# Another order for the opening of an attention and MLP kernel, with the first MLP weight loaded in four places

## Chip, cores and metric

One core of one Trainium2 chip runs the whole program. The metric is the device time of one execution in microseconds; the lower, the better. Shown for the kernel before are three runs: 415.26, 416.80 and 418.37 us, median 416.8 us.

## What is computed

Per batch and head: q and k are divided by their root mean square along the 64 dimensions and weighted by a gain; the scores are their products over 8; a softmax and a product with v follow. The heads are laid side by side (768 columns), and an MLP with a leaky activation ends the work.

```python
def rmsnorm(x, g):
    return x / np.sqrt(np.mean(x * x, axis=-1, keepdims=True) + 1e-06) * g
# q, k, v: (8, 12, 448, 64)
scores = 1/8 * np.matmul(rmsnorm(q, g_q), rmsnorm(k, g_k).transpose(0, 1, 3, 2))
attn = softmax(scores)
x = np.matmul(attn, v).transpose(0, 2, 1, 3).reshape(3584, 768)
h = x @ w_in                                      # 768 x 2048
g = np.maximum(h, 0.0) + alpha * np.minimum(h, 0.0)
out = g @ w_out                                   # 2048 x 768
```

## The kernel before, in words

Attention goes in 24 units, three for each of the eight batches; a unit `y` holds two heads of each half of the heads (the text says "unit 3" for y = 3, "q3" and "k3" for its inputs). The MLP goes batch by batch: 16 column blocks of 128 of the first weight (`up(b,ft)`, `slope`, `larger`), then output tiles of 128 tokens (`down` and, from tile 6, a scheme with fewer products).

For units 0 to 8 the steps of one unit, each on a fixed engine, are: `load_qk(y)` on the queue of SyncE (SP); `square` on GpSimd (POOL; L382, unit 0 and q1 on ScalarE); `reduce` on VectorE (DVE; L401); `root`, two short ScalarE (ACT) instructions (L422, L423); `scale` (L442, on VectorE for units 1, 2 and q3, else on GpSimd); `turn`, 14 transposes on TensorE (PE; L566) and two copies out of PSUM on VectorE (L573, L575); seven `score` steps (L594, four matmuls each in the early units) and seven `soft` (the exponential, L608, 0.8 to 0.9 us each on ScalarE); `den`, `log`, `invert` (the sum of the exponentials and its reciprocal), `attend` (the product with v, L619) and `times` (L715). `follow` is a one-column copy on GpSimd. `spin` is matmuls without use for the result.

`load_w_in(c)` issues from GpSimd four loads of 32 partitions by 512 columns (L345) for column quarter c, and, for c = 0 and c = 2, four more loads with rows 512 to 767 of a column half (L353). So column blocks 0 to 3 need load_w_in(0), blocks 4 to 7 need load_w_in(0) and (1), blocks 8 to 11 need load_w_in(2), blocks 12 to 15 need load_w_in(2) and (3). `begin(ft)` does the part of `up(0,ft)` that needs only units 0 and 1. `load_v` and `load_w_out` are issued by GpSimd as well.

The order of everything is written out by hand in one string, `PLAN`: the steps are emitted in its order, and each engine runs its own instructions in that order. Where an instruction waits, all behind it on its engine wait. The GpSimd loads are numbered round robin over eight completion semaphores (DMASW0 to DMASW7 in the built program): a load waits until the load eight places before it on that queue has landed. The loads of SP go round robin over eight others in the same way.

Buffers: q and k of units 0, 1, 3, 4, 6, 7 lie in four rotating buffers (`nat`), so load_qk(3) waits for the last reader of unit 0's, which is `scale`; units 2, 5 and 8 share one place in `arena`. v has one buffer. PSUM has two score buffers, one spare buffer (a last argument 1 in `score`, `up`, `den`, `down` and others changes which of them is taken) and two single banks for the MLP and the transposes.

Of the kernel before, what the change touches and what calls it, by code (L numbers as in the profile page):

```python
# [32 lines left out]
reduce(2,q,1) soft(0,3) score(0,1,0) scale(1,k) scale(1,q) soft(0,4) score(0,2,0) soft(0,2)  # L33
reduce(2,k) score(0,6,1) turn_one(1,q) soft(0,1) turn_one(1,k) score(1,0,1) score(1,3,0) spin(1)
score(1,2,0) soft(0,6) root(2) soft(1,0) load_qk(4) soft(1,3) scale(2,k) scale(2,q) soft(1,2)
score(0,5,1) score(1,1,0) soft(0,5) soft(1,1) score(1,5,0) turn(2) soft(1,5) score(1,6,1)
soft(1,6) reduce(3,q,None) score(1,4,0) score(2,0,0) square(3,k) soft(1,4) den(0+1,0) follow(1,k)
# [3 lines left out]
times(0+1,0,0) turn(3) score(2,5,0) square(4,k) load_qk(6) reduce(4,q,None) soft(2,3) soft(2,2)  # L41
soft(2,5) den(2,0) log(2) reduce(4,k,None) invert(2) attend(2,0,1) score(3,0,1) square(5,q)
square(5,k) times(2,0,0) score(3,1,0) begin(0) reduce(5,q) square(6,q) soft(3,0) begin(1)
up(0,0,0) load_w_out(0) reduce(5,k) up(0,1,0) begin(2) begin(3) root(4) up(0,2,0) up(0,3,1)
up(0,4,0) scale(4,q) slope(0,0) soft(3,1) larger(0,0) score(3,2,0) score(3,6,0) slope(0,1)
load_qk(7) follow(2,k) larger(0,1) slope(0,4) slope(0,2) slope(0,3) larger(0,4) up(0,5,0)
larger(0,2) larger(0,3) root(5) soft(3,6) slope(0,5) soft(3,2) larger(0,5) up(0,6,0) scale(4,k)
turn(4) scale(5,q) up(0,8,0) score(4,0,0) slope(0,6) score(4,1,1) square(6,k) larger(0,6)
slope(0,8) score(3,5,0) up(0,9,0) load_w_out(1) scale(5,k) soft(4,0) square(7,q) larger(0,8)
up(0,11,0) load_qk(8) score(4,2,0) score(3,3,0) soft(3,5) load_v(1) square(7,k) up(0,7,1)  # L50
soft(4,1) slope(0,9) up(0,10,0) reduce(6,q) square(8,q) reduce(6,k) load_w_out(2) soft(4,2)
up(0,12,0) slope(0,11) larger(0,9) soft(3,3) score(3,4,0) slope(0,10) score(4,3,0) larger(0,11)
larger(0,10) slope(0,7) larger(0,7) up(0,13,0) soft(3,4) slope(0,12) larger(0,12) turn(5)
up(0,14,0) square(8,k) soft(4,3) score(4,6,0) slope(0,13) score(4,4,1) root(6) slope(0,14)
larger(0,13) up(0,15,0) scale(6,q) reduce(8,q) soft(4,4) score(5,4,0) larger(0,14) scale(6,k)
score(5,0,1) reduce(7,q) slope(0,15) larger(0,15) down(1,0,0) score(5,2,1) score(4,5,0) soft(4,6)
soft(5,0) soft(5,4) soft(5,2) score(5,1,0) soft(4,5) down(0,0,0) turn(6) load_w_out(3) den(3+4,1)
reduce(7,k) attend(3+4,0,0) score(5,5,0) score(5,6,0) soft(5,1) mix_weights(0,1) log(3+4)
invert(3+4) soft(5,5) soft(5,6) mix_weights(0,3) attend(3+4,1,0) score(6,0,1) score(5,3,0)
soft(6,0) score(6,4,0) down_end(0,0) down(2,0,0) soft(5,3) root(7) scale(7,q) load_qk(9) soft(6,4)  # L60
scale(7,k) den(5,0) attend(5,0,1) down_end(1,0) mix_weights(0,2) times(3+4,0,0) times(3+4,1,0)
times(3+4,1,1) load_qk(10) log(5) down(0,1,0) reduce(8,k) invert(5) down_end(2,0) times(5,0,1)
times(5,0,0) times(5,0,3) times(5,0,2) score(6,5,1) mix_weights(0,0) score(6,1,0) down_end(0,1)
score(6,6,0) soft(6,5) turn(7) up(1,1,1) square(9,q) down(1,1,0) root(8) reduce(9,q) soft(6,6)
score(6,3,1) score(7,0,0) slope(1,1) score(6,2,0) up(1,2,0) up(1,0,0) soft(6,1) soft(7,0)
soft(6,3) square(9,k) up(1,3,1) up(1,4,0) slope(1,2) slope(1,0) larger(1,1) down_end(1,1)
reduce(9,k) root(9) larger(1,2) load_qk(11) larger(1,0) slope(1,3) scale(8,q) soft(6,2) up(1,7,0)
slope(1,4) larger(1,3) larger(1,4) scale(8,k) score(7,4,0) slope(1,7) larger(1,7) up(1,5,1)
scale(9,q) turn(8) score(7,5,0) soft(7,4) score(7,1,0) up(1,6,0) square(10,q) slope(1,5)
larger(1,5) up(1,10,0) soft(7,5) soft(7,1) up(1,8,1) scale(9,k) up(1,9,0) reduce(10,q)  # L70
score(7,2,0) slope(1,6) slope(1,10) larger(1,6) mix_weights(1,1) score(7,6,0) slope(1,8)
slope(1,9) soft(7,6) up(1,12,1) up(1,11,0) soft(7,2) square(10,k) up(1,13,0) larger(1,8)
larger(1,10) slope(1,12) score(7,3,0) larger(1,9) up(1,14,1) slope(1,11) slope(1,13)
# [1030 lines left out]
```

## Time and profile before

| | |
|---|---|
| median of three runs | 416.8 us |
| the profiled execution | 416.01 us |
| its span in the trace | 414.2 us, so 1.81 us lie around it |
| PE busy in the span | 397.6 us (96%) |
| DVE, ACT, POOL busy | 267.9, 269.9, 301.2 us |
| first score matmul | 14.43 us |
| begin(0), the first MLP matmul | 45.06 us |
| mean granted TensorE clock | 0.988 |

Times inside an execution are microseconds from the start of the span. In the timeline, a line is: start, duration, engine, source line, operation, output<-inputs, count; what stands in brackets is the idle time of that engine just before, and what ended it. In the table of stretches a line gives the length, then busy time and count for PE, PEld (weight loads), DVE, ACT and POOL, then the granted TensorE clock, the busy share of the 16 DMA engines and GB/s. The chain of waits is the work that ended last, followed back: start, length, what.

### The profile page before, as it was taken

To read this page: it belongs to the slowest core of one execution; us is meant where nothing else is said; L and a number is where in the kernel's file an instruction comes from. 1 tells how busy PE (TensorE), PEld (TensorE's weight loads), DVE (VectorE), ACT (ScalarE), POOL (GpSimd) and SP (SyncE) were. 2 spreads that over 40 slices of the span, in tenths; PEclk is the share of its full clock that TensorE was granted. 3 is DMA by queue.
4 is the path that set the end of the run, shared out by engine and by line. 5 is a ranking of instruction groups with operands and counts; after the bars stand their busy time and mean duration, and the time that the engine had idled before them with its cause. 6 is when DMAs were issued, how large, how long until landed. Compare 5 with 4: busy or idle time off the path is not lost.

```text
span 414.2 us, 11992 instructions
## 1 busy us (share of the span) xinstructions
PE 397.6 (96%) x5083; PEld 211.3 (51%) x5083; DVE 267.9 (65%) x479; ACT 269.9 (65%) x405; POOL 301.2 (73%) x200
## 2 busy tenths in 40 slices
PE   7785999999999999999999999999999999999995
PEld 3342444555445555555455445545555455655664
DVE  3936776566766777677867758886659545654422
ACT  5594688757786776667897887876875885235110
POOL 7849998297888698998695996489497709600780
PEclk9897999999999999999999999999999999999999
DMA  8999599697867594749872695794707000230143
GB/s 254 244 273 167 111 245 188 128 234 189 161 133 185 147 216 99 174 117 200 212 172 58 157 218 147 151 217 106 161 21 143 24 0 23 59 78 0 34 101 95
DMA packets 37221, 58.39 MB, mean 141 GB/s; under 512 B 4768, under 2 KB 28976, under 8 KB 37168
## 3 DMA queue, kind: packets, MB, share of 16 engines
q1 hardware_dynamic: 23232, 45.43, 42.9%
q0 software_dynamic: 13536, 11.81, 19.3%
q8 instruction: 39, 0.64, 0.7%
q10 hardware_dynamic: 400, 0.39, 0.3%
q14 instruction: 14, 0.11, 0.1%
HBM read 58.40 MB, written 11.01 MB: 168 GB/s over the span
## 4 chain that ended last, share of the span: by engine, by line
PE 89%; DMA 4%; POOL 3%; DVE 2%; ACT 1%; issue 1%; POOLq 0%
PE hT L732 26%; PE hTa L732 9%; PE sc L594 8%; PE op L798 7%; PE qx L860 5%; PE av L619 5%; PE qc L860 4%; PE qz L860 4%; PE oq L860 3%; PE dn L619 3%; PE qxa L860 3%; DMA w_in_sb<-in_moe_w_in_dram 2%; PE avb L619 2%; PE oqm L860 2%; DMA nat<-in_q_dram 1%; PE tps L566 1%
## 5 line engine op out<-in xcount | busy, mean ns | idle before, releaser
L608 ACT ACTIVATE expT<-sc 128x896 f16<-128x896 f32 x168 | 146.1, 916 | 41.7 <-PE sc L594 39.9
L732 PE MATMUL hT<-xT,w_in_sb 128*128 128x448 f16 x558 | 115.7, 353 | 0.3 <-DVE xT L715 0.2
L732 PEld LDWEIGHTS <-w_in_sb 128*128 128x128 f16 x768 | 73.0, 98 | 73.1 <-issue 8.8
L429 POOL TENSOR_TENSOR qs<-nat,rr 128x896 f16<-128x896 f32 x30 | 65.6, 2218 | 26.7 <-ACT rr L423 23.2
L772 ACT ACTIVATE gT<-hT,cols 128x448 f16<-128x448 f32 x92 | 58.4, 635 | 39.6 <-PE hT L732 38.5
L778 DVE TENSOR_TENSOR gT<-hT,gT 128x448 f16<-128x448 f32 x93 | 57.4, 620 | 38.0 <-ACT gT L772 37.2
L594 PE MATMUL sc<-qT,kT 64*32 64x448 f16 (+1 forms) x1092 | 50.1, 359 | 8.2 <-ACT expT L608 6.6
L371 POOL TENSOR_TENSOR nat<-nat 128x896 f32<-128x896 f32 x30 | 50.6, 1694 | 8.8 <-DVE gT L778 4.4
L860 PEld LDWEIGHTS <-gT 128*128 128x128 f16 x352 | 33.4, 98 | 25.5 <-issue 4.1
L732 PE MATMUL hTa<-xT,w_in_sb 128*128 128x448 f16 x198 | 42.9, 353 | 0.0
L715 DVE TENSOR_TENSOR xT<-av,rden 64x448 f16<-64x448 f32 (+1 forms) x37 | 27.2, 736 | 12.9 <-ACT rden L677 6.9
L594 PEld LDWEIGHTS <-kT 64*32 64x32 f16 (+1 forms) x1092 | 16.8, 94 | 36.7 <-issue 27.8
L848 POOL TENSOR_TENSOR gs<-gT 128x1024 f16<-128x1024 f16 x4 | 8.5, 2126 | 36.7 <-DVE gT L778 36.7
L392 DVE TENSOR_REDUCE sp<-nat 128x28 f32<-128x896 f32 x30 | 32.1, 1071 | 2.0 <-DMA nat<-in_k_dram 2.0
L798 PE MATMUL op<-w_out_sb,gT 128*128 128x384 f16 x176 | 30.3, 326 | 0.2 <-DVE xT L715 0.2
L772 ACT ACTIVATE gT<-hTa,cols 128x448 f16<-128x448 f32 x33 | 21.0, 635 | 10.5 <-PE hTa L732 10.0
L778 DVE TENSOR_TENSOR gT<-hTa,gT 128x448 f16<-128x448 f32 x33 | 20.4, 619 | 10.6 <-ACT gT L772 10.2
L619 PEld LDWEIGHTS <-vt 64*32 64x32 f16 x1344 | 19.6, 92 | 12.4 <-issue 2.6
L798 PEld LDWEIGHTS <-gT 128*128 128x128 f16 x192 | 18.3, 98 | 14.5 <-issue 3.0
L619 PE MATMUL av<-expT,vt 64*32 64x448 f16 x896 | 24.3, 350 | 0.0
L856 POOL TENSOR_TENSOR gT<-gT 128x1024 f16<-128x1024 f16 x11 | 23.4, 2131 | 0.0
L860 PEld LDWEIGHTS <-arena 128*128 128x128 f16 x136 | 12.6, 98 | 10.5 <-issue 2.3
(152 smaller groups left out, 575.4 us busy)
## 6 DMA issues: line engine op xcount, KB each, us to landing
nat<-in_q_dram SPq DMA_DIRECT2D x60, 216.0 KB, 4.0
nat<-in_k_dram SPq DMA_DIRECT2D x60, 216.0 KB, 5.1
out_dram<-osb SPq DMA_DIRECT2D x107, 96.0 KB, 3.2
vt<-in_v_dram POOLq DMA_DIRECT2D x8, 672.0 KB, 8.2
w_in_sb<-in_moe_w_in_dram POOLq DMA_DIRECT2D x24, 128.0 KB, 7.1
w_out_sb<-in_moe_w_out_dram POOLq DMA_DIRECT2D x4, 768.0 KB, 8.2
nat<-in_k_dram SPq DMA_DIRECT2D x6, 448.0 KB, 6.2
nat<-in_q_dram SPq DMA_DIRECT2D x5, 448.0 KB, 6.3
```

Of the source, the lines that this page charges most:

```text
L371: nc.gpsimd.tensor_mul(out=sqs[y, nm], in0=t[:, :, :HD], in1=t[:, :, :HD])
L392: nc.vector.tensor_reduce(out=parts[y][:, ts("qk".index(nm), 4 * J), :1], in_=sqs[y, nm], axis=AXIS_X, op=ALU.add,)
L429: nc.gpsimd.tensor_mul(out=t.rearrange("p j d n -> p n j d"), in0=nat[y, nm][:, :, :HD].rearrange("p (n j) d -> p n j d", j=J), in1=r.unsq ...
L594: nc.tensor.matmul(out=sc[ds(64 * g + m * c, m), par, :S].rearrange("p (j c) -> p j c", j=J), lhsT=kT[ds(64 * par, 64), j, g, ts(c, m)], r ...
L608: nc.scalar.activation(out=expT[y][:, j], in_=scs[y, j][:, :, :S], func=AF.Exp, scale=QK_SCALE, bias=EXP_BIAS,)
L619: nc.tensor.matmul(out=accs[g][ds(32 * n, 32), :S], lhsT=weights(g, y, par, c, j), rhs=expT[y][ds(64 * g, 64), j, par, :], start=(j == 0), ...
L715: nc.vector.tensor_mul(out=o, in0=p, in1=q)
L732: nc.tensor.matmul(out=hT[:, :S], lhsT=w_in_sb[:, block_of(g, i), ts(ft, 128)], rhs=xT[b][:, g, i, :], start=(i == 0 and g == 0), stop=(i ...
L772: nc.scalar.activation(out=g, in_=hT[:, :S], func=AF.Copy, scale=alpha_sb[:, ft : ft + 1])
L778: nc.vector.tensor_max(out=g, in0=hT[:, :S], in1=g)
L798: nc.tensor.matmul(out=op[:, :OH], lhsT=gT[:, ft, ts(tile % J, 128)], rhs=w_out_sb[:, ft, ts(oh, OH)], start=(ft == 0), stop=(ft == NF - 1),)
L860: nc.tensor.matmul(out=bank[:, c], lhsT=g[:, ft], rhs=v[:, ft, c], start=(first and ft == 0), stop=(ft == HF - 1), skip_group_check=True,)
```

## The change

Only `PLAN` changes. Both strings hold the same 1324 steps with the same arguments, apart from the bank argument. The order of the first 49 lines (up to slope(1,13), in the MLP of batch 1) is another; the rest keeps its order, with 17 bank arguments changed. In the four load_w_in, what stands between them in GpSimd's order is:

- before: load_w_in(1), square(1,k), load_v(0), follow(0,k), square(2,q), square(2,k), load_w_in(0), load_w_in(2), square(3,q), square(3,k), follow(1,k), load_w_in(3), scale(3,k), square(4,q), square(4,k), square(5,q), square(5,k), square(6,q), load_w_out(0), scale(4,q), ...
- after: load_w_in(1), square(1,k), load_v(0), square(2,q), follow(0,k), load_w_in(3), square(2,k), follow(1,k), square(3,q), square(3,k), square(4,q), load_w_in(0), scale(3,k), square(5,q), square(5,k), square(4,k), load_w_in(2), scale(4,q), scale(4,k), square(7,q), load_w_out(0), load_w_out(1), follow(2,k), scale(5,k), load_v(1), square(6,q), load_w_out(2), scale(5,q), load_w_out(3), ...

SP loads the units in the order 3, 4, 5, 7, 6, 8, 9, 10 in place of 3 to 10. The four mix_weights(0,p) go from between turn(6) and turn(7) to behind turn(8). The new string is one line shorter, so line numbers behind it are one lower.

```diff
-opening() part_square(q,0:1,0:7,act) part_square(q,1:2,0:7,act) part_reduce(q,0:1,0:7) spin(2,0)
-part_reduce(q,1:2,0:7) part_root(q,0:7) part_square(k,0:2,0:3,act) part_scale(q,0:7,7,pool)
-part_reduce(k,0:2,0:3) part_square(k,0:2,3:7,act) square(1,q) load_w_in(1) spin(1)
-part_reduce(k,0:2,3:7) part_root(k,3:7) reduce(1,q) square(1,k) part_root(k,0:3) gains()
-part_turn(q,r0-7) load_qk(3) spin(1,0) part_scale(k,0:3,3,vec) part_turn(k,r0-3)
-part_scale(k,3:7,4,vec) part_copy(q,0:7,vec) part_turn(k,r3-7) load_v(0) reduce(1,k) follow(0,k)
-square(2,q) part_copy(k,0:3,vec) part_copy(k,3:7,vec) root(1) square(2,k) score(0,0,0) soft(0,0)
-reduce(2,q,0) score(0,4,1) load_w_in(0) load_w_in(2) square(3,q) score(0,3,0) spin(1)
...
-soft(2,0) log(0+1) load_qk(5) score(2,1,0) spin(1) reduce(3,k,0+1) attend(0+1,1,0) score(2,6,0)
-score(2,4,1) attend(0+1,0,1) soft(2,1) root(3) score(2,3,1) invert(0+1) scale(3,q) score(2,2,0)
-load_w_in(3) soft(2,4) soft(2,6) times(0+1,1,0) times(0+1,1,1) scale(3,k) square(4,q)
...
+opening() part_square(q,0:1,0:7,act) part_reduce(q,0:1,0:7) spin(2,0) part_square(q,1:2,0:7,act)
+part_reduce(q,1:2,0:7) load_qk(3) part_root(q,0:7) part_square(k,0:2,0:3,act)
+part_reduce(k,0:2,0:3) part_scale(q,0:7,7,pool) part_square(k,0:2,3:7,act) part_reduce(k,0:2,3:7)
+load_w_in(1) square(1,k) part_root(k,0:3) spin(1) part_scale(k,0:3,3,vec) square(1,q) load_qk(4)
+part_root(k,3:7) reduce(1,q) gains() part_turn(k,r0-3) part_turn(q,r0-7) part_scale(k,3:7,4,vec)
+load_v(0) square(2,q) part_copy(q,0:7,vec) reduce(1,k) part_copy(k,0:3,vec) part_turn(k,r3-7)
+part_copy(k,3:7,vec) score(0,0,0) score(0,3,0) root(1) follow(0,k) score(0,4,1) scale(1,q)
+load_w_in(3) scale(1,k) reduce(2,q,0) score(0,6,0) soft(0,0) turn_one(1,q) turn_one(1,k) soft(0,4)
+score(0,1,1) score(1,0,0) spin(1) score(0,5,0) soft(0,6) square(2,k) soft(0,3) score(1,3,1)
+score(0,2,1) reduce(2,q,1) score(1,1,0) soft(0,1) follow(1,k) reduce(2,k) soft(1,0) score(1,5,0)
+square(3,q) soft(1,3) reduce(3,q,None) spin(1) root(2) square(3,k) scale(2,q) soft(0,5) spin(1,0)
+score(1,6,1) score(1,2,0) soft(0,2) soft(1,1) soft(1,5) reduce(3,k,0+1) scale(2,k) turn(2)
+square(4,q) load_w_in(0) soft(1,6) root(3) soft(1,2) score(1,4,0) spin(1) score(2,0,1) scale(3,k)
+soft(1,4) score(2,1,0) load_qk(5) den(0+1,1) soft(2,0) soft(2,1) square(5,q) score(2,6,1) log(0+1)
+score(2,3,0) soft(2,6) attend(0+1,1,0) attend(0+1,0,1) invert(0+1) scale(3,q) times(0+1,1,0)
+soft(2,3) score(2,2,1) times(0+1,1,1) score(2,4,0) times(0+1,0,0) reduce(4,q,None) turn(3)
+score(2,5,1) soft(2,2) square(5,k) reduce(5,q) soft(2,4) soft(2,5) den(2,1) attend(2,0,1) log(2)
+invert(2) square(4,k) times(2,0,0) reduce(4,k,None) score(3,0,1) soft(3,0) load_qk(7) score(3,2,0)
+begin(0) begin(1) reduce(5,k) begin(2) root(4) up(0,0,0) up(0,1,0) begin(3) load_qk(6) slope(0,0)
+load_w_in(2) up(0,2,0) larger(0,0) scale(4,q) slope(0,1) soft(3,2) up(0,4,0) up(0,3,1) larger(0,1)
+up(0,5,0) score(3,6,0) slope(0,3) scale(4,k) square(7,q) load_w_out(0) larger(0,3) slope(0,4)
+slope(0,2) load_w_out(1) score(3,1,0) larger(0,2) larger(0,4) soft(3,6) soft(3,1) slope(0,5)
+root(5) turn(4) up(0,6,0) score(3,4,0) slope(0,6) score(4,0,0) up(0,10,1) soft(3,4) follow(2,k)
...
```

More of the change, by code (lines that the diff above doesn't have):

```diff
@@ L31 @@
-square(2,q) part_copy(k,0:3,vec) part_copy(k,3:7,vec) root(1) square(2,k) score(0,0,0) soft(0,0)
-reduce(2,q,0) score(0,4,1) load_w_in(0) load_w_in(2) square(3,q) score(0,3,0) spin(1)
[L33 to L36, printed above, removed]
@@ L43 @@
[L43 to L48, printed above, removed]
@@ L49 @@
[L49 to L72, printed above, removed]
@@ new lines @@
+reduce(6,q) soft(4,6) larger(0,13) slope(0,14) up(0,15,0) soft(5,6) score(5,5,1) score(4,5,0)
+reduce(6,k) slope(0,15) score(5,4,0) load_qk(9) soft(4,5) larger(0,14) larger(0,15) root(6)
+reduce(7,k) square(8,q) down(0,0,0) score(5,1,1) score(5,2,0) score(4,4,0) soft(5,5) soft(5,4)
+load_qk(10) soft(5,2) down(1,0,0) scale(6,q) scale(6,k) soft(5,1) root(7) soft(4,4) reduce(8,q)
+turn(6) down_end(1,0) den(3+4,1) attend(3+4,0,1) down_end(0,0) score(5,3,1) square(8,k) log(3+4)
+score(6,0,0) soft(5,3) attend(3+4,1,0) down(2,0,1) den(5,1) invert(3+4) attend(5,0,1) scale(7,k)
@@ new lines @@
+soft(6,0) times(3+4,0,0) times(3+4,1,0) reduce(8,k) root(8) times(3+4,1,1) scale(7,q) score(6,6,1)
+down_end(2,0) log(5) score(6,5,0) down(0,1,0) invert(5) times(5,0,3) times(5,0,0) soft(6,5)
+scale(8,q) soft(6,6) times(5,0,1) score(6,4,1) times(5,0,2) score(6,1,0) down_end(0,1)
+score(6,2,0) soft(6,4) turn(7) soft(6,2) soft(6,1) square(9,q) up(1,1,1) down(1,1,0) score(7,0,0)
+slope(1,1) larger(1,1) up(1,0,1) reduce(9,q) slope(1,0) up(1,2,0) scale(8,k) soft(7,0) square(9,k)
+down_end(1,1) reduce(9,k) up(1,3,0) slope(1,2) up(1,4,1) larger(1,0) up(1,7,0) score(7,4,0)
```

41 lines of the change are left out of this document (25 added, 16 removed).

## The prediction, made before the changed kernel was timed

> **What bounds the kernel now.** I read the stretches first, to see where PE is not full, then GpSimd's timeline there, then the chain of waits that leads out of it. The stretches:
>
> ```profile
> 25.00:30.00 5.00, 4.11 (x91) 1.97 (x94) 0.75 (x2) 4.97 (x7) 2.15 (x4) 1.00 1.12 260
> 30.00:35.00 5.00, 3.19 (x119) 1.69 (x104) 2.04 (x3) 0.18 (x1) 4.45 (x6) 1.00 1.09 227
> 35.00:40.00 5.00, 2.38 (x21) 1.54 (x21) 3.65 (x6) 4.51 (x7) 4.99 (x6) 0.60 0.85 116
> 40.00:45.00 5.00, 5.00 (x128) 2.16 (x126) 2.99 (x4) 2.45 (x3) 5.00 (x4) 0.72 0.58 187
> 45.00:50.00 5.00, 5.00 (x31) 2.57 (x28) 4.42 (x6) 3.45 (x7) 4.98 (x6) 1.00 0.33 33
> 150.00:200.00 50.00, 50.00 (x668) 26.57 (x666) 37.77 (x72) 34.77 (x52) 46.64 (x26) 1.00 0.72 155
> ```
>
> From 45 us on PE is busy almost without a break at full granted clock, so the end moves by as much as begin(0), at 45.06, moves, unless PE is made to wait behind it. Between 30 and 45 us PE is idle or at a granted clock of 0.60 to 0.72. GpSimd's timeline before that:
>
> ```profile
> 16.15 2.21 POOL L345 DMA_DIRECT2D w_in_sb<-in_moe_w_in_dram  x4
> 18.36 1.60 POOL L353 DMA_DIRECT2D w_in_sb<-in_moe_w_in_dram  x3
> 20.75 0.53 POOL L353 DMA_DIRECT2D w_in_sb<-in_moe_w_in_dram  x1 [0.80 <-DMA vt<-in_v_dram]
> ...
> 26.88 0.54 POOL L345 DMA_DIRECT2D w_in_sb<-in_moe_w_in_dram  x1 [2.23 <-DMA w_in_sb<-in_moe_w_in_dram]
> ...
> 31.08 3.46 POOL L382 TENSOR_TENSOR nat<-nat 128x896 f32<-128x896 f32 x3
> ```
>
> The sixteen loads of load_w_in(0) and (2) hold GpSimd from 16.15 to 31.08. Sixteen issues of 0.54 are 8.6 us; the other 6.3 us are waits, each for the load eight places before. Unit 3's squares stand behind them, at 31.08. What waited, in ScalarE's and PE's timelines and the chain:
>
> ```profile
> 35.23 0.23 ACT L422 ACTIVATE rr<-ss 128x28 f32<-128x28 f32 x1 [5.04 <-DVE ss L401]
> ```
> ```profile
> 37.40 0.59 PE L594 MATMUL sc<-qT,kT 64*64 64x448 f16 x4 [4.21 <-ACT expT L608]
> 38.73 1.67 PE L566 MATMUL tps<-ident,arena 128*128 128x128 f16 x14
> 40.85 2.45 PE L619 MATMUL dn<-expT,ones 64*32 64x448 f16 x56
> ```
> ```profile
> 31.08 3.47 POOL nat L382 x3
> 34.55 0.02 issue
> 34.57 0.63 DVE ss L401
> 35.20 0.02 issue
> 35.23 0.23 ACT rr L422
> ```
>
> Squares, reduce, root(3): ScalarE stood 5.04 us before root(3), PE 4.21 us behind ScalarE. The granted clock then was 0.50 from 36 to 42.6, and turn and den took 1.67 and 2.45 in place of 0.95 and 1.56 (the same lines at 23.93 and 26.85).
>
> **The change, part by part.** I walk the new order of each queue with these rows' durations, from where it parts from the old. Everything up to begin(0) is the same work in both orders, four units turned and 23 score steps, so begin(0) compares like with like.
>
> GpSimd. Unchanged to 11.4 (scale of q0, load_w_in(1), square(1,k)). Then load_v(0) 0.90 to 12.3; square(2,q) in halves 1.8 to 14.1; follow 0.15; load_w_in(3) 2.2 to 16.45. Square(2,k) at 1.67 ends 18.1, square(3,q) 19.9. Square(3,k) needs k3. Its landing is not in the record; SP issues it at 12.15, and the loads issued at 17.22 and 18.21 took 6.8 and 10.2, so it lands at 19.0 to 22.4. I take 20.7, nearer the earlier end as its queue is shorter: squares end 22.5. Square(4,q) needs q4: issued at 16.2 behind scale(1,q), at the 6.8 of its old load landed at 23.0, at 10.2 at 26.4; the first, as it is the same load a microsecond earlier: 23.5 to 25.2. Load_w_in(0), eight issues at 0.54, to 29.5. It waits for load_v(0) (landed 20.5 before, issued at the same time) and load_w_in(3); the four loads behind v before landed 21.4 to 26.6, and the last is wanted at 29.0, so no wait. Scale(3,k) ends 31.2, square(5,q) 32.9, square(5,k) 34.5, square(4,k) 36.2, load_w_in(2) 40.5.
>
> Opening of the others. ScalarE squares k0 before q1 now, VectorE's reduce(1,q) and gains come behind the first scale: gain waits for square(1,k) on GpSimd to 11.46, scale of k0's second part ends 12.1, PE's transposes of q 12.85, VectorE's copy 13.4, reduce(1,k) 14.4, copy of k 14.8. First score 14.8 against 14.43, a loss of 0.4. The two parts of reduce and turn that were reordered in front of that end no later than before.
>
> ScalarE from there, at 0.82 per soft: soft(0,0) at 15.1, four more to 19.2, soft(1,0) 20.0, 0.5 us idle behind a spin (0.95), soft(1,3) 21.4, root(2) 0.47, four to 25.2, soft(1,6) 26.0, root(3) 0.47 (its reduces end 24.7, so no wait), soft(1,2), (1,4), (2,0), (2,1) to 29.8, log 30.7, (2,6) 31.5, invert 32.4, four softs with 0.35 idle to 36.0. PE: den(2) 0.4 behind the last soft, attend(2) 1.45 to 37.9, two scores, begin(0) at 38.4. Turn(3) stands in this chain at 33.7; scale(3,k) has ended 31.2. Gain: 45.06 - 38.4 = 6.66. As a check, the parts: 5.04 of ScalarE's wait, 1.2 + 1.5 of ScalarE's idle time at 40.98 and 43.44 behind the slow PE, less 0.4 at the first score, less some 0.7 of new short waits, 6.6.
>
> VectorE beside GpSimd. Gain is one column and took 0.85, ending with the square on GpSimd; scale at 15.75 beside a square took 1.40 against 1.09 without. So a VectorE product of two SBUF tensors can wait for the rest of the GpSimd instruction, at most 1.67. GpSimd's issues did not cost it anything (1.09 at 35.74). With squares now running at 16.5 to 25.2, scale(2,q) and scale(2,k), at 21.95 and 24.1, meet them: 0.55 and 0.55, so turn(2) ends 26.7 in place of 25.6, and behind it 0.2 reaches soft(2,0). Bounds: nothing, since ScalarE is full there, and twice 1.67 = 3.3; I take 0.2, as the walk places them. [...]
>
> Behind begin(0). PE would run to up(0,10), the first block of load_w_in(2), at 48.3 (begin(0) to (3) 3.0, up(0,0) to (0,5) 3.8, four score steps 1.0, turn(4) 0.8, up(0,6) 1.13, and the 0.2). Load_w_in(2) is issued 36.2 to 40.5; landings of such loads ran from 3.6 (little else moving) to 10.2: 44.1 to 50.7 for the last. As only two q/k loads run beside it I take some 5.5: 46.0, cover 2.3. Load_w_in(0), last issued 29.5, lands by 39.7 at the worst, wanted at 38.4 for its first half (issued by 27.4, landed by 37.6) and at 40.7 for its second. Scale(4,k) ends 44.3, turn(4) wants it at 45.8; scale(5,q) 54.8, turn(5) at 56.4; both hidden, with 1.5 us of cover. SP: load 7 ahead of 6 waits for unit 3's scale, q6 then leaves at 42.6 and is squared at 50.5; no cost with landings of 6.3. Mix_weights(0,p), four of 1.62, move behind turn(8), where GpSimd had 8.49 idle before 83.48 and 23.2 in all before L429: nothing; if that cover were gone, up to 6.5 of GpSimd's time. The 17 changed banks lie where PE never waits; a wrong one costs one release, a soft of 0.9. All waits of PE behind 55 us are 0.6, so the gain is at most that, and several misses cost 2; I take 0.1.
>
> Sum against the profiled execution: 416.0 - 6.66 + 0.2 + 0.1 = 409.7. It was 0.8 below the median of the three runs; from 416.8 the same gain gives 410.4. I predict 410.0.
>
> **The rivals.** (a) The waits on loads come back at both pauses of eight: load_w_in(0) waits if load_w_in(3) lands later than 27.4 for its first. Before, eight such issues took 9.5 (21.59 to 31.08) in place of 4.3. With 5.2 more at each pause, scale(3,k) ends 36.4, 2.7 behind turn(3)'s want, and with a slow clock for 2 us more begin(0) is at 43.3; the second 5.2 puts scale(4,k) at 54.7, 4 behind turn(4), and 2 again for the clock: 416.0 - 1.7 + 6 = 420.3. It turns into a loss from about 3 us at each pause. For it: the same rotation of eight, and landings of 10.2. Against: thirteen microseconds between load_w_in(3) and the load that waits for it. (b) Load_w_in(2) lands at 10.2 after its issue: up(0,10) waits 2.4 to 3, and a slow clock costs up to 1.7 (half of 3.4): 412.5 to 414.5, about 413.5. For it: the cover is only 2.3. (c) VectorE behind GpSimd and a slow clock in the opening cost 1.5 to 2 more: 411.5. (d) The time is given back behind the opening, by a wait of PE on GpSimd's scale or on banks, near all of it: 416. Against it: GpSimd waits for others 23.2 at L429, and PE was full from 150 to 250. That the change does not do what it says, that is, loads still wait, is (a).
>
> **How the numbers follow.** Forecast 0.62 (408 to 412), (c) 0.12, (b) 0.12, (d) 0.06, (a) 0.08. Three runs of this kernel spread by 0.7%, so about 1% is what a measurement can tell: 412.6 and 421.0. Faster is forecast and (c), 0.74. (a) at 420.3 is 1% over the profiled execution, just at the bound: I give slower 0.05 and leave 0.03 with (b) and (d) in the same, 0.21. The range 407.5 to 414.5 takes in (b) and (c) and leaves out (a), (d) and a little of the forecast, 0.18.
>
> **What would show it.** Right: GpSimd issues load_w_in(0) and (2) in 4 to 5 us each without idle time; unit 3's squares before 23; no wait of ScalarE above 1 us between 20 and 36; granted clock 1.00 from 30 on; begin(0) at 38 to 39; PE without gaps behind. Wrong: idle time ended by a load in GpSimd's rows (a); PE waiting at hTa or hT for w_in (b); VectorE scales of 1.4 and more followed by PE waits (c); begin(0) early, the span not (d).

## The result, and the profile after

The changed kernel takes 423.0 us (median of four runs, 420.67 to 424.77), the kernel before on the same chip 416.34; the ratio is 1.0149, with a 95% interval of 1.0111 to 1.0187. It is slower by 6 to 7 us where 6 to 7 us less was forecast. The medians in this document are of all executions; the ratios leave out an execution that lies more than 1.5% above the fastest of its kernel. The profiled execution took 422.41 us, its span is 420.2, so 2.2 lie around it.

Two numbers divide the span: where begin(0), the first MLP matmul, starts, and what is left from there to the end.

| | begin(0) | from begin(0) to the end |
|---|---|---|
| before | 45.06 | 369.1 |
| forecast | 38.4 | 369.5 |
| after | 44.86 | 375.3 |

So the gain in the opening did not come (6.5 us short), and the rest lost 5.8 that the forecast did not have. Both have to be explained. The stretches of the changed kernel (columns as in the table of stretches above):

```profile
25.00:30.00 5.00, 3.37 (x31) 1.07 (x23) 3.44 (x5) 4.48 (x7) 4.26 (x6) 0.84 0.36 77
30.00:35.00 5.00, 5.00 (x92) 2.69 (x84) 3.29 (x4) 4.29 (x7) 3.84 (x6) 0.81 1.12 222
35.00:40.00 5.00, 5.00 (x162) 2.85 (x146) 2.06 (x3) 4.73 (x7) 2.08 (x2) 1.00 1.08 306
40.00:45.00 5.00, 4.05 (x126) 1.88 (x126) 3.20 (x5) 3.27 (x4) 5.00 (x7) 1.00 0.31 58
45.00:50.00 5.00, 5.00 (x28) 2.56 (x27) 4.62 (x6) 3.31 (x7) 3.90 (x6) 1.00 1.09 173
80.00:85.00 5.00, 1.95 (x49) 0.53 (x30) 1.09 (x1) 1.19 (x2) 0.00 (x0) 0.81 1.07 231
150.00:200.00 50.00, 50.00 (x655) 26.75 (x653) 36.44 (x70) 34.88 (x53) 46.62 (x27) 1.00 0.76 163
```

Between 30 and 40 PE is full now, as forecast, where it was idle for 4.4 of the ten; its granted clock is 0.81 from 30 to 35, where 1.00 was given as a sign of being right. New is the hole at 80: PE is busy 1.95 of 5. GpSimd's timeline of the changed kernel:

```profile
14.98 2.22 POOL L344 DMA_DIRECT2D w_in_sb<-in_moe_w_in_dram  x4
17.20 1.69 POOL L381 TENSOR_TENSOR arena<-arena 128x896 f32<-128x896 f32 x1
20.99 0.19 POOL L512 COPY mark<-arena 128x1 f16<-128x1 f16 x1 [2.09 <-DVE arena L441]
21.13 3.46 POOL L381 TENSOR_TENSOR nat<-nat 128x896 f32<-128x896 f32 x3
25.74 1.68 POOL L381 TENSOR_TENSOR nat<-nat 128x896 f32<-128x896 f32 x1 [1.15 <-issue]
27.36 2.19 POOL L344 DMA_DIRECT2D w_in_sb<-in_moe_w_in_dram  x4
29.54 2.13 POOL L352 DMA_DIRECT2D w_in_sb<-in_moe_w_in_dram  x4
42.40 2.22 POOL L344 DMA_DIRECT2D w_in_sb<-in_moe_w_in_dram  x4
44.59 2.15 POOL L352 DMA_DIRECT2D w_in_sb<-in_moe_w_in_dram  x4
```

The loads do what they should: eight issues in 4.3 to 4.4 us from 27.36 and from 42.40, with no idle time ended by a load. But follow(1,k) at 20.99 waited 2.09 for scale(1,k) on VectorE, and VectorE's timeline says why it was late:

```profile
17.76 3.10 DVE L441 TENSOR_TENSOR arena<-nat,rr 128x896 f16<-128x896 f32 x2
26.76 1.60 DVE L441 TENSOR_TENSOR qs<-arena,rr 128x896 f16<-128x896 f32 x1 [1.56 <-ACT rr L422]
29.34 1.08 DVE L441 TENSOR_TENSOR qs<-arena,rr 128x896 f16<-128x896 f32 x1
```

The two scales of unit 1 took 3.10, where alone they take 1.08 each (as at 29.34). The first ran from 17.76 to 19.86: square(2,k) on GpSimd ended at 18.90, and the scale 0.96 behind it. PE, first in the opening, then around 80 us:

```profile
11.28 0.21 PE L1030 MATMUL ct<-ident,arena 18*128 18x18 f32 x1 [3.28 <-DMA arena<-in_g_k_dram]
16.93 0.39 PE L490 MATMUL tps<-ident,qs 128*128 128x128 f16 x4 [2.03 <-DVE kT L500]
41.78 1.32 PE L618 MATMUL dn<-expT,ones 64*32 64x448 f16 x47 [0.95 <-issue]
```
```profile
79.50 1.12 PE L618 MATMUL avb<-expT,vt 64*32 64x448 f16 x34
83.67 1.32 PE L618 MATMUL avb<-expT,vt 64*32 64x448 f16 x22 [3.05 <-issue]
84.92 3.55 PE L797 MATMUL opa<-w_out_sb,gT 128*128 128x384 f16 x16
```

A product with v, 56 matmuls on data that is there since the first of them, stops after 34 for 3.05 us. The releaser is "issue": no semaphore, no other engine. The granted clock falls to 0.50 for 3.4 us there, from 83.1 (the `down` behind took 3.55; 2.77 in a kernel without the stop, below). The same happened in the middle of den(2), 0.95 before 41.78, after 9 of 56 matmuls. Further on, two more waits of PE are new, and short:

```profile
211.45 0.73 PE L731 MATMUL hTa<-xT,w_in_sb 128*128 128x448 f16 x3 [0.41 <-ACT expT L607]
```
```profile
337.99 1.30 PE L731 MATMUL hT<-xT,w_in_sb 128*128 128x448 f16 x6 [0.45 <-DVE gT L777]
```

### The profile page after: what moved, and what is told of

Read it like the earlier page. It is cut to its first block, busy times and chain, and to the rows that moved or that the text cites. A ratio compares the mean times of both kernels' runs of the same rounds, so it can differ in the third digit from the quotient of the medians.

```text
span 420.2 us, 11986 instructions
## 1 busy us (share of the span) xinstructions
PE 401.1 (95%) x5083; PEld 211.8 (50%) x5083; DVE 269.7 (64%) x479; ACT 270.4 (64%) x405; POOL 301.6 (72%) x200
## 4 chain that ended last, share of the span: by engine, by line
PE 92%; DVE 2%; DMA 2%; ACT 2%; issue 1%; POOL 1%; POOLq 0%
PE hT L731 24%; PE hTa L731 10%; PE sc L593 9%; PE op L797 6%; PE av L618 5%; PE qx L859 5%; PE qz L859 4%; PE qc L859 4%; PE oq L859 3%; PE dn L618 3%; PE qxa L859 3%; PE avb L618 3%; PE oqm L859 2%; DMA arena<-in_g_k_dram 2%; PE tps L565 2%; PE spin L1005 2%
## 5 line engine op out<-in xcount | busy, mean ns | idle before, releaser
L731 PE MATMUL hT<-xT,w_in_sb 128*128 128x448 f16 x546 | 113.6, 353 | 0.6 <-DVE gT L777 0.5
L731 PEld LDWEIGHTS <-w_in_sb 128*128 128x128 f16 x768 | 72.9, 98 | 74.1 <-issue 9.9
L777 DVE TENSOR_TENSOR gT<-hT,gT 128x448 f16<-128x448 f32 x91 | 56.1, 619 | 38.4 <-ACT gT L771 37.9
L731 PE MATMUL hTa<-xT,w_in_sb 128*128 128x448 f16 x210 | 45.5, 353 | 0.4 <-ACT expT L607 0.4
L777 DVE TENSOR_TENSOR gT<-hTa,gT 128x448 f16<-128x448 f32 x35 | 21.7, 620 | 10.9 <-ACT gT L771 10.5
L797 PE MATMUL op<-w_out_sb,gT 128*128 128x384 f16 x160 | 27.5, 327 | 0.2 <-DVE xT L714 0.2
```

The source lines that it names most:

```text
L731: nc.tensor.matmul(out=hT[:, :S], lhsT=w_in_sb[:, block_of(g, i), ts(ft, 128)], rhs=xT[b][:, g, i, :], start=(i == 0 and g == 0), stop=(i ...
L777: nc.vector.tensor_max(out=g, in0=hT[:, :S], in1=g)
L797: nc.tensor.matmul(out=op[:, :OH], lhsT=gT[:, ft, ts(tile % J, 128)], rhs=w_out_sb[:, ft, ts(oh, OH)], start=(ft == 0), stop=(ft == NF - 1),)
```

## The experiments

Fourteen kernels; "the repeat" (a0) is the changed kernel itself, run once more beside the first ones. In the kernels of the experiments the plan is wrapped into fewer lines, so that their line numbers are 5 below those of the changed kernel (6 below those of the kernel before). For ten of them, the two numbers of the traces (one traced execution each); the other four, b1, b3, a3 and e2, are told where they stand:

| run | median us | ratio to before | begin(0) | begin(0) to the end |
|---|---|---|---|---|
| a0: repeat of the changed kernel | 421.81 | 1.0140 (1.0100 to 1.0179) | 43.31 | 376.4 |
| c2: square(2,k) behind follow(1,k) | 420.95 | 1.0104 (1.0055 to 1.0153) | 40.13 | 378.5 |
| c1: turn ahead of copy | 423.56 | 1.0168 (1.0137 to 1.0199) | 43.16 | 377.8 |
| a2: opening of before | 419.90 | 1.0083 (1.0051 to 1.0115) | 40.34 | 376.1 |
| a1: loads of units 9, 10 late | 415.75 | 0.9980 (0.9953 to 1.0006) | 43.28 | 370.1 |
| b2: before, these loads early | 420.82 | 1.0104 (1.0068 to 1.0140) | 45.27 | 373.5 |
| a4: load_w_out(3) late | 423.94 | 1.0181 (1.0144 to 1.0219) | 43.09 | 376.7 |
| e1: only the load of 10 late | 422.90 | 1.0153 (1.0112 to 1.0194) | 44.03 | 376.7 |
| d1: c2 and a1 | 412.97 | 0.9931 (0.9897 to 0.9965) | 40.03 | 370.0 |
| d2: d1 and the old banks | 412.06 | 0.9894 (0.9863 to 0.9926) | 40.79 | 368.7 |

The last column of this table falls into two groups: 368.7 to 370.1 where the loads of units 9 and 10 go out late, 373.5 to 378.5 where the load of 9 goes out early.

**The repeat (a0).** No edit.

> The changed kernel unaltered, for its spread and a second trace. If its loss is its own and not one execution's: time 1.01 to 1.02 of before, PE stands about 3 us at 80 inside the group avb with no releaser named, begin(0) at 44 to 46. If the late landing of the gains (ct at 11.28, against 9.64 before) was chance, ct stands near 9.6 here and begin(0) 1 to 2 us earlier.

Measured: 421.81. The stop is there again, 3.32 us at 79.07, and that in den(2), 0.85 at 39.37. The matmul `ct` started at 9.45 in place of 11.28, so the late landing of g_k belonged to the one execution. In four more traced executions with the same order up to begin(0) (this one and, below, a1, a4 and e1), `ct` starts at 9.45 to 10.43 and begin(0) lies at 43.09 to 44.03, against 44.86. That the late g_k makes the whole difference fits, but is not shown: within the four, begin(0) does not follow `ct`. What follows is compared with the repeat.

### The opening

**A square moved from beside the scales (c2).**

```diff
 ... score(0,5,0) soft(0,6)
-square(2,k)
 soft(0,3) score(1,3,1) score(0,2,1) reduce(2,q,1) score(1,1,0) soft(0,1) follow(1,k)
+square(2,k)
 reduce(2,k) ...
```

> The changed kernel with one step moved: square(2,k) on GpSimd behind follow(1,k) in place of ahead of it, so that no GpSimd square runs beside the scales of unit 1 on VectorE. Theory (a VectorE product of two SBUF tensors waits for the GpSimd instruction that runs): the scales of unit 1 take 2.1 in place of 3.1 to 4.2, the turns of unit 1 and unit 3's squares come 0.3 to 2 earlier, begin(0) 0.5 to 1.5 earlier than 43.3, about 420.5 to 421.5. Rival (the scales take as long whatever GpSimd does; or the contention meets the scales of unit 2 instead): the scales of unit 1 as long as before, or those of unit 2 longer by what unit 1 gains, and 421.8.

Measured: 420.95. VectorE's scales of unit 1, and PE from den(2) to begin(0):

```profile
15.69 2.08 DVE L436 TENSOR_TENSOR arena<-nat,rr 128x896 f16<-128x896 f32 x2
```
```profile
34.98 0.55 PE L613 MATMUL dn<-expT,ones 64*32 64x448 f16 x9
37.04 1.33 PE L613 MATMUL dn<-expT,ones 64*32 64x448 f16 x47 [1.51 <-issue]
40.13 1.69 PE L726 MATMUL hT<-xT,w_in_sb 128*128 128x448 f16 x8
```

The scales take 2.08 in place of 4.17 in the repeat, and begin(0) comes 3.2 us earlier, at 40.13, from this one step, where 0.5 to 1.5 were expected. The other traces agree: 40.03 to 40.88 with the square moved (c2, d1, d2, e2), 43.09 to 44.86 in the changed kernel and in a0, a1, a4 and e1. The chains that ended last show the way, first the repeat, then c2:

```profile
15.40 4.18 DVE arena L436 x2
19.62 0.93 PE tps L513 x7
21.58 1.75 PE spin L1000 x2
```
```profile
17.17 1.60 PE tps L513 x14
19.60 0.95 PE spin L1000 x2
```

The scales are in the repeat's chain, PE's transposes of unit 1 wait for them, and PE then works at a granted clock of 0.50; GpSimd is in neither chain. The granted clock is 0.50 for 3.4 us ahead of it (10.2 in the repeat). 1.51 us of what is left is the stop in den(2), so without it begin(0) would be at 38.6. The total hardly moved, since PE now stopped a second time, 3.21 us at 84.13 beside 3.06 at 75.89: the theory holds for the opening, and the time is given back behind it.

**The turn ahead of the copy (c1).**

```diff
-part_copy(k,0:3,vec) part_turn(k,r3-7)
+part_turn(k,r3-7) part_copy(k,0:3,vec)
```

> The changed kernel with one step moved: part_turn(k,r3-7) ahead of part_copy(k,0:3), as the kernel before has it. Theory (in the opening PE waits for VectorE's copy because the turn of k's second part writes the same PSUM tile that the copy is reading): PE's wait of 2.0 to 2.7 for kT goes, the first score comes 0.4 to 1.2 earlier than 14.9, begin(0) 0.5 to 1.2 earlier than 43.3, about 421. Rival (the wait only shows when the copy ends, and the copy of k is what the score needs anyway): first score and time as in the changed kernel, 421.8.

Measured: 423.56. The first score comes at 14.64 against 14.89, begin(0) at 43.16 against 43.31. PE still waits 1.59 for VectorE's kT; the first score gained 0.25 of the 0.4 to 1.2 that were expected, and begin(0) 0.15. That is near what the rival said, but the test is not a clean one: the scales of unit 1 took 4.99 here and ended at 19.88, against 4.17 and 19.57 in the repeat, which hides a gain of 0.25 ahead of them.

**The opening of the kernel before (a2).** Up to score(0,0,0) the steps of the kernel before, square(2,k) at its later place, load_qk(4) behind load_v(0); then the changed kernel, less a spin(1,0) that the opening already has.

```diff
-opening() part_square(q,0:1,0:7,act) part_reduce(q,0:1,0:7) spin(2,0) part_square(q,1:2,0:7,act) ...
+opening() part_square(q,0:1,0:7,act) part_square(q,1:2,0:7,act) part_reduce(q,0:1,0:7) spin(2,0) ...
 ... score(0,0,0) ...
```

> The changed kernel with the opening of the kernel before up to score(0,0) (part_turn of k's second part ahead of the copy of its first part, scales behind gains), square(2,k) and all behind it in the new order. Theory 3: the new order of the opening cost 2 to 2.5 us (first score at 17.25 against 14.43), of which half comes through to begin(0): begin(0) at 42.5 to 44, time 1 to 2 us less than the changed kernel. Rival: the late first score came from the late landing of the gains alone, which no order sets: first score as late as in the unaltered changed kernel of this set, time the same.

Measured: 419.90, begin(0) at 40.34, 2 us earlier than the theory gave, scales of unit 1 in 2.08, two stops of 3.03 and 1.07 between 76 and 87. The first score lies at 14.63, against 14.89 in the repeat, which has the new order, so the 17.25 of the first execution was not the order's alone; in that the rival was right. The old opening gives the same 3 us as the one square of c2: follow(0,k) and root(1) come earlier in it, and the scales are through before the square begins.

### The stop at 80 us

**The loads of units 9 and 10 late (a1).** In the changed kernel SP issues them from 72.9 and 78.4, in the kernel before from 80.1 and 86.4, behind the first stores of the output.

```diff
-... score(5,4,0) load_qk(9) soft(4,5) ... score(4,4,0) soft(5,5) soft(5,4) load_qk(10) soft(5,2) ...
+... score(5,4,0) soft(4,5) ... score(4,4,0) soft(5,5) soft(5,4) soft(5,2) ...
+... scale(7,q) load_qk(9) ... times(5,0,3) load_qk(10) ...
```

> The changed kernel with load_qk(9) and load_qk(10) moved back, behind scale(7,q) and times(5,0,3), as they stood before. Theory 1: PE's stand of 3.05 us at 80.6, in the middle of a group of matmuls, is PE's own instructions coming late: they come as packets of 16 KB on queue 8 through the DMA engines, which were full of w_out and of units 9 and 10 (share 1.25). With units 9 and 10 out of the way the stand falls below 1 us and the half clock behind it goes: 4 to 5 us less than the changed kernel, about 418. Rival 2: it is a bank or a transfer of v or w_out that the profile doesn't name: the stand stays, time unchanged within 1 us.

Measured: 415.75, 6.1 us less than the repeat, where 4 to 5 were expected. PE's timeline, no stop:

```profile
77.92 1.63 PE L613 MATMUL avb<-expT,vt 64*32 64x448 f16 x56
79.48 2.77 PE L792 MATMUL opa<-w_out_sb,gT 128*128 128x384 f16 x16
```

What PE waited for, as I read it, is in the table of DMA queues of the changed kernel (packets, MB, share):

```profile
q8 instruction: 39, 0.64, 0.7%
```

39 packets of 16384 bytes. At the stops (in den(2), at 80.6, and a third of 0.23 at 90.2) PE had started 705, 1729 and 1985 recorded instructions, matmuls and weight loads but for some 15: 1024 and 256 apart. PE's 10166 recorded matmuls and weight loads come to 261 for each of the 39 packets. From these numbers I take queue 8 as PE's and a packet as 256 of its instructions, an estimate. The packet at 62 to 67 us starts when PE is near 1256 in all of them (1245 to 1270), and in the kernel before the next starts at 1509. So I take a packet as due when PE starts number 1512:

```
                    PE at 1512   packet          late by   PE stands
before                 77.16     77.08 - 78.25     -0.1       -
after                  77.19     81.16 - 82.37      4.0      3.05
a0 (repeat)            75.64     79.54 - 80.79      3.9      3.32
a1 (loads late)        75.61     76.36 - 77.31      0.8       -
b2 (before, early)     77.37     80.73 - 82.05      3.4      2.54
a4 (w_out(3) late)     75.42     79.69 - 80.99      4.3      3.59
e1 (only 10 late)      76.35     80.51 - 81.79      4.2      3.42
d2                     73.23     73.93 - 74.89      0.7       -
```

In c2, a2 and c1, worked out the same way, the packet is late by 3.9, 3.6 and 4.4, with stops of 3.06, 3.03 and 3.62.

PE goes on 1.30 us behind the end of the packet in the changed kernel (82.37 to 83.67), 1.33 in den(2) (40.45 to 41.78).

**The kernel before with these loads early (b2).**

```diff
 ... scale(6,k)
+load_qk(9) load_qk(10)
 ... scale(7,q)
-load_qk(9)
 ... times(3+4,1,1)
-load_qk(10)
```

> The kernel before with only the loads of units 9 and 10 moved, both directly behind scale(6,k). Theory A (it takes the pile of load_w_in(2), load_w_out and load_v together with these loads to delay PE's instructions; in the kernel before the weights land sooner): no stand of PE above 1 us between 70 and 95, 415.5 to 417. Theory B (these loads alone delay PE's instructions, whatever else moves): a stand of 2 to 3.5 us with the releaser issue between 74 and 90, 418 to 421.

Measured: 420.82, 4.5 us more than the kernel before, with only these two steps moved. PE's and SP's timelines:

```profile
79.64 1.30 PE L613 MATMUL avb<-expT,vt 64*32 64x448 f16 x41
83.48 0.57 PE L613 MATMUL avb<-expT,vt 64*32 64x448 f16 x15 [2.54 <-issue]
```
```profile
68.18 1.75 SPq L321 DMA_DIRECT2D nat<-in_q_dram  x4
70.03 1.85 SPq L321 DMA_DIRECT2D nat<-in_k_dram  x4
88.30 1.73 SPq L321 DMA_DIRECT2D nat<-in_q_dram  x4
```

The load of unit 10 got out at 88.30 only, against 86.38 in the kernel before, so what came early is the load of unit 9 alone. Theory B holds, and for one load: issued from 68 on, it goes with a packet that is 3.4 late, without the late load_w_in(2) that I had held for a part of the cause.

**load_w_out(3) late (a4).**

```diff
-load_qk(8) slope(0,12) load_w_out(3) larger(0,12) ... turn(6) down_end(1,0)
+load_qk(8) slope(0,12) larger(0,12) ... turn(6) load_w_out(3) down_end(1,0)
```

> The changed kernel with only load_w_out(3) moved to behind turn(6), where the kernel before has it: eight transfers less in the pile ahead of 80 us, the loads of units 9 and 10 as early as in the changed kernel. Theory A (the pile as a whole delays PE's instructions): the stand of 3.05 to 3.3 shrinks to under 1.5, and the time is 417 to 420. Theory B (the loads of units 9 and 10, which SyncE issues just ahead, do it alone): the stand stays at 3, the time at 421 to 423, or more if down(0,0) then waits for load_w_out(3).

Measured: 423.94, 0.9 above the range of theory B, a stop of 3.59. Theory A, that the pile as a whole does it, falls for the second time. The share of the DMA engines from 75 to 80 us is 1.14 here and 1.20 in the changed kernel, against 0.29 before and 0.53 in a1:

```profile
75.00:80.00 5.00, 5.00 (x160) 2.88 (x166) 3.62 (x6) 2.38 (x3) 0.00 (x0) 1.00 0.29 45
```
```profile
75.00:80.00 5.00, 5.00 (x180) 2.52 (x157) 2.25 (x5) 3.07 (x4) 2.94 (x2) 1.00 0.53 110
```

So the packet of 77 finds the engines nearly free where the loads come late. Full engines alone are not enough, though: the packet at 66.58 of the changed kernel came at its place in a stretch with a share of 1.17.

**Only the load of unit 10 late (e1).**

```diff
-... soft(5,4) load_qk(10) soft(5,2) ...
+... soft(5,4) soft(5,2) ... times(5,0,3) load_qk(10) ...
```

> The changed kernel with only the load of unit 10 moved, behind times(5,0,3); the load of unit 9 stays early. Theory (each load in flight when an instruction packet is due delays that packet; the load of 9 is in flight when the packet of 77 is due): the stand of about 3.3 in avb at 79 stays, that packet still 3 us or more late, the one after it no longer, and no second stand or one below 0.3: 420.5 to 422. Rival (it takes both loads together): the stand shrinks below 1.5, 416 to 419.

Measured: 422.90, 0.9 above the range that was given, but with the stops as expected: 3.42 at 79.78, and no second one. So the load of unit 9 is enough to delay the packet of 77, as in b2. The repeat has no second stop either, so that is no sign of what the load of unit 10 does; the packet behind is. Counted from PE's number 1768 it is 3.1 to 5.3 late in the six kernels with the load of unit 10 early (after, a0, a4, c1, c2, a2), 0.3 to 1.2 in those where it goes out later (before, b2, a1, d2, e1).

### The kernel before with one part of the change

**Only load_w_in(2) moved (b1).**

```diff
-score(0,4,1) load_w_in(0) load_w_in(2) square(3,q)
+score(0,4,1) load_w_in(0) square(3,q)
-square(4,k) load_qk(6)
+square(4,k) load_w_in(2) load_qk(6)
```

> The kernel before with one step moved: load_w_in(2) from behind load_w_in(0) to behind square(4,k). Theory of the prediction (the sixteen loads in a row cost ScalarE 5.04 and PE 1.6 more): no ScalarE wait of 5 us, begin(0) at 38.5 to 40 in place of 45.06, time about 410 to 411. Rival: the load moved on collides with w_out and v behind it as in the changed kernel, PE stands without a named releaser at 70 to 85 or waits for w_in: 414 to 418.

Measured: 415.76 (ratio 0.9973, 0.9936 to 1.0009). ScalarE's 5.04 is gone and begin(0) is at 39.09, 6 us earlier: the first step of the prediction is right by itself. Then PE waits, and what is late next is VectorE, in its timeline:

```profile
46.40 1.29 PE L726 MATMUL hT<-xT,w_in_sb 128*128 128x448 f16 x6 [2.60 <-DVE gT L772]
```
```profile
43.10 1.09 DVE L395 TENSOR_REDUCE ss<-arena 128x14 f32<-128x896 f32 x1 [2.62 <-POOL arena L376]
```

VectorE stood 2.62 for the square of unit 5, which stood on GpSimd behind the eight loads of load_w_in(2); larger(0,0) stood behind VectorE's reduce, and PE behind that. From begin(0) to the end b1 takes 374.9, 5.8 more than the kernel before; the 2.60 and 3.4 us of half clock behind it (47.7 to 51.1) make up the larger part, the rest is not broken down.

**The squares of unit 5 ahead of the loads (b3).**

```diff
-load_w_in(0) load_w_in(2) square(3,q)
+load_w_in(0) square(3,q)
-scale(3,k) square(4,q) ... square(4,k) ... square(5,q) square(5,k) ... square(6,q) load_w_out(0) ... scale(4,k)
+square(4,q) square(4,k) scale(3,k) ... square(5,q) square(5,k) load_w_in(2) ... scale(4,k) square(6,q) load_w_out(0)
```

> The kernel before with load_w_in(2) behind square(5,k), the squares of unit 4 ahead of scale(3,k), and square(6,q) with load_w_out(0) behind scale(4,k). Theory (the kernel before with only load_w_in(2) moved to behind square(4,k) got ScalarE's 5.04 back and lost it again because reduce(5) waited for unit 5's squares behind eight loads; with those squares ahead of the loads it keeps it): begin(0) at 38.5 to 39.5, PE without a wait of 2.6 behind it, 410 to 412. Rival 1 (load_w_in(2), issued at 40, stands in the transfers of load_w_out(0) to (2) and v(1) and lands late, or PE's instructions come late): waits of PE between 45 and 80, 414 to 417. Rival 2 (scale(3,k) comes too late behind the squares of unit 4): PE waits 1 to 3 us for it ahead of turn(3), and begin(0) at 40 to 42.

Measured: 415.11 (ratio 0.9960, 0.9926 to 0.9994), begin(0) at 42.86. PE stood 2.65 in front of turn(3), as rival 2 said, with begin(0) 0.9 later than it gave; the time is that of rival 1; the mechanism was in neither. VectorE and GpSimd:

```profile
30.82 5.44 DVE L436 TENSOR_TENSOR arena<-nat,rr 128x896 f16<-128x896 f32 x1 [2.16 <-ACT rr L417]
36.18 1.14 DVE L709 TENSOR_TENSOR xT<-avb,rden 128x448 f16<-128x448 f32 x2
```
```profile
28.70 3.32 POOL L376 TENSOR_TENSOR nat<-nat 128x896 f32<-128x896 f32 x2
31.98 1.68 POOL L436 TENSOR_TENSOR arena<-nat,rr 128x896 f16<-128x896 f32 x1
33.63 4.16 POOL L376 TENSOR_TENSOR arena<-arena 128x896 f32<-128x896 f32 x2
```

A scale of 1.09 stood for 5.44: it began at 30.82 beside a square, and three GpSimd products in a row (ends 32.02, 33.66, 35.30) went ahead of it; it ended at 36.25, 0.95 behind the third. The GpSimd square behind that took 2.47 in place of 1.67.

### Together

**Old opening and late loads (a3).** The edits of a2 and a1.

```diff
-(the opening of the changed kernel, load_qk(9) behind score(5,4,0), load_qk(10) behind soft(5,4))
+(that of the kernel before, load_qk(9) behind scale(7,q), load_qk(10) behind times(5,0,3))
```

> The changed kernel with both edits: the opening of the kernel before up to its first score, and the loads of units 9 and 10 behind scale(7,q) and times(5,0,3). Theory (two separate losses: one in the opening, one where PE's own instructions come late behind full DMA engines at 79 us): the gains add, 421.8 less 6.0 less 1.9, about 414 (413 to 415), with begin(0) at 40.3 and no stand of PE above 1 us between 70 and 95. Rival (both edits only shift the same queue of transfers, and the stand comes back as the work moves forward): a stand of 2 to 3 us between 70 and 90, and 416 to 419.

Measured: 413.11, ratio 0.9919 (0.9891 to 0.9946): in the time the two gains add, as the theory said. The one execution that was traced took 419.11, the other six 411.52 to 414.6, so its trace does not stand for them, and that begin(0) and the stop went as the theory said is not shown here.

**The square and the late loads (d1), and the old banks (d2).**

```diff
-soft(0,6) square(2,k) soft(0,3) ... load_qk(9) ... load_qk(10)
+soft(0,6) soft(0,3) ... follow(1,k) square(2,k) ... scale(7,q) load_qk(9) ... times(5,0,3) load_qk(10)
```
```diff
-qb2(8,0) ... up(3,2,1) ... up(6,10,0) ... qc2(20,1)
+qb2(8,1) ... up(3,2,0) ... up(6,10,1) ... qc2(20,0)
```

> The changed kernel with square(2,k) behind follow(1,k) and the loads of units 9 and 10 behind scale(7,q) and times(5,0,3): no other step differs. Theory (the opening loses by GpSimd squares beside VectorE's scales of unit 1, the middle by PE's instructions that come late when the loads of 9 and 10 join transfers that already fill the DMA engines): begin(0) at 39.5 to 40.5, no stand of PE above 1.2 us between 70 and 95; the square alone gave begin(0) 3.5 us earlier and then stands of 3.06 and 3.21, the loads alone took 6 us: 421.8 less 6 less 3.5 is 412.3 (411 to 413.5). Rival (work that arrives 3.5 us earlier runs into the same full DMA engines all the same): stands of 2 to 3 us stay between 70 and 90, and 414 to 417.

> The kernel of the run beside it with the 17 changed PSUM banks set back to those of the kernel before. Theory (two of them make PE wait, 0.41 for ScalarE at 207 and 0.45 for VectorE at 333): both waits go, 0.8 to 0.9 less than the run beside it. Rival (the waits stand in for others that are hidden behind them): the time of the run beside it.

Measured: 412.97 and 412.06. Three steps moved in the changed kernel turn 1.4% more into 0.7% less. With the old banks both waits, at 201 and 327 in d1, are gone from the trace; the medians differ by 0.9 as the theory said, but the executions of each kernel scatter by more (411.79 to 416.48 and 410.43 to 413.64), so the 0.9 rests on the two waits. d2 is faster than both kernels, 0.9894 of the kernel before. Its row for 75 to 80 us:

```profile
75.00:80.00 5.00, 5.00 (x112) 2.65 (x112) 2.73 (x4) 2.65 (x4) 0.86 (x1) 1.00 0.72 175
```

**The load of unit 7 held (e2).** In d2 the stop in den(2) is 1.50; the load of unit 7 goes out at 29.2, just ahead of the packet.

```diff
-soft(2,3) score(2,2,1) ... soft(3,0) load_qk(7) score(3,2,0)
+soft(2,3) load_qk(7,hold) score(2,2,1) ... soft(3,0) score(3,2,0)
```

> The kernel with the square behind follow(1,k), the late loads of 9 and 10 and the old banks (412.06, stand of 1.50 in den(2) at 36.2), with the load of q7 held behind soft(2,3) by a one-column copy on ScalarE, so that the loads of unit 7 go out at about 34 in place of 29.2 and 31.9. Theory (the loads of unit 7 in flight when the packet of 32 is due make it 3 us late, and PE stands 1.5 in den(2)): the packet at 32 to 33, the stand below 0.4, begin(0) at 39.2 to 39.7, 410.5 to 411.2. Rival (the eight loads of load_w_in(0), issued 25.8 to 30.1, delay it, whatever SyncE does): packet still at 34.5 to 35, the stand stays at 1.5, 412.

Measured: 412.60, ratio 0.9911 (0.9877 to 0.9946), a stop of 0.78, begin(0) at 40.88. The loads of unit 7 went out at 35.0, and the packet came at 35.36 all the same, 2.7 behind PE's number 492, as in d2 (3.0) and in the kernel before (2.8, where PE stood for ScalarE and lost nothing by it). The theory falls for this packet. That the eight loads of load_w_in(0) delay it would fit b1, where four loads were issued there and it was late by 0.8; but b3 issued four there too (26.49 to 28.69) and its packet, at 34.03, was 3.1 late. What delays this packet stays open.

## Why the prediction was wrong

**The loads (rival (a)).** Right: load_w_in(0) and (2) are issued in 4.3 us each without a wait, and rival (a) did not happen.

**ScalarE's 5.04 and begin(0) at 38.4.** The wait is gone, and with the one square moved the walk holds to 1 us in d2: load_w_in(0) begins at 25.81 (walk 25.2), scale(3,k) ends at 31.83 (31.2), load_w_in(2) begins at 36.68 (36.2), and begin(0) less the stop is at 39.3 (38.4). In c2 begin(0) less the stop is at 38.6, closer, while GpSimd runs 2 us behind its walk (27.45, 33.47, 38.31), which cost PE nothing there. In the changed kernel the step failed, for the next reason.

**"VectorE beside GpSimd", 0.2.** The first term that failed. The walk priced only the scales of unit 2 and left out those of unit 1, though by its own times scale(1,k) meets a square: scale(1,q) has ended at 16.2, where q4 is issued behind it, and square(2,k) runs from 16.45 to 18.1. In the run the scales of unit 1 began at 17.76 (15.40 in the repeat), beside the square, and took 3.10 (4.17). The term measured 3.2 (43.31 against 40.13). That this is close to the upper bound of 3.3 is luck, as the bound was for the scales of unit 2: 2.1 of it is the longer scales of unit 1, and the rest fits PE's half clock behind them, 10.2 us of it in the repeat against 3.4 in c2 (the chains above). The bound of a single wait was wrong as well: "the rest of the GpSimd instruction, at most 1.67" became 4.35 in b3 (5.44 less 1.09). Where one GpSimd product ran beside it, the scale ended 0.96 behind that product (19.86 against 18.90 in the changed kernel); where GpSimd's products stood back to back, in b3, VectorE waited for three of them and ended 0.95 behind the third.

In the kernel before, the second scale of unit 1 ran in 1.08 at 17.07 beside load_w_in(0)'s issues; in the new order square(2,k) stands there. Its scales of unit 2 ran in 1.09 and 1.08 between GpSimd's waits for its loads, but that cover was not needed: in c2, beside squares, they take 1.09 and 1.08 too.

**"Behind begin(0)", 0.1.** The second term, and as large: 5.8 above the forecast, 6.2 above the kernel before. 5.3 of the 6.2 fall ahead of up(1,1), 50.94 from begin(0) against 45.63; the changed kernel, then the kernel before:

```profile
95.80 1.30 PE L731 MATMUL hTa<-xT,w_in_sb 128*128 128x448 f16 x6
```
```profile
90.69 1.30 PE L732 MATMUL hTa<-xT,w_in_sb 128*128 128x448 f16 x6
```

Load_w_in(2) landed in time and PE did not wait for scale(4,k), as said; load 7 ahead of 6 cost PE nothing either, though q6 left at 49.55 and not at 42.6 as the walk had it. What failed is that the moved loads of units 9 and 10, issued 7 to 8 us earlier, were priced nowhere, while the packets of queue 8, which I take for PE's instructions, come through the DMA engines that these loads use: the packet due at 77 was 4.0 late in the changed kernel, 0.8 in a1. Taking them back gained 6.1 (a1); moving them alone in the kernel before, where only unit 9's came early, cost 4.5 (b2).

**"The 17 changed banks lie where PE never waits".** Wrong by two waits, 0.41 and 0.45, which are gone where the banks are set back (d2).

**Sum.** 409.7 + 6.5 (begin(0)) + 5.8 (behind) + 0.4 (2.2 around the span in place of 1.8) = 422.4, the profiled execution. Of the 6.5, 1.5 is the difference of this execution from the repeat, 3.2 the square beside the scales, and the last 1.7 (40.13 against 38.4) is for the most part the stop in den(2), 1.51 in c2.

**The rivals.** (d), time given back behind the opening, names the place, but its waits on GpSimd's scale or on banks are 0.9 of it; its 416 and the chance of 0.06 were both too small. (c) names the mechanism of the opening, at half its price. The one case on the losing side, (a), was not what happened.

## What to carry to other kernels

Before work of GpSimd is moved, list which VectorE products run at its new place: a product of two SBUF tensors waited for three GpSimd products in a row (5.44 in place of 1.09 in b3). Count a moved load not only by what waits for it but by what else goes through the DMA engines when it is issued, PE's instructions included: a stop of 3.05 inside a group of equal matmuls, with the releaser "issue", was the sign here. And when a large reordering loses, put single steps back in the new kernel: three of 1324 steps put back or moved, and the banks, made up for all of it.

## What the runs showed of the hardware

- Queue 8 brought 39 packets of 16384 bytes in a run; by the 261 recorded matmuls and weight loads for each, and stops that lie 1024 and 256 of them apart, I take one as 256 of PE's instructions, an estimate. In stretches of small matmuls they were used up quickly: 56 matmuls with their weight loads took 1.52 us. A packet that came 3.4 to 4.4 us late cost 2.5 to 3.6 us of standing. The granted clock then fell to 0.50 for 3.4 us, in a0 and e1 for 6.8, in c2 only behind the second stop.
- The loads that delayed it were SyncE's, of 216 KB each, issued 4 to 9 us before the packet was due. Why a packet is late beside these and on time beside GpSimd's weight loads at 66 us was not found out.
- A VectorE scale of 1.09 took 5.44 beside three GpSimd products in a row. In the repeat and in c1 the first scale of unit 1 took 1.68 and 2.50, with only GpSimd's load issues beside their first 1.3 and 2.1 us; in c2, beside the same issues, 1.08; in e2 a scale of unit 3 took 2.61 so. That difference is open.
